# Moving the release points of streamed weights in the recurrent attention layer (layer A)

## The chip, the cores and the metric

The kernel runs on one core of a Trainium2 chip. The metric is the device time of one execution in microseconds (us). Three timed runs of the kernel before gave 3307.75, 3314.41 and 3315.86 us; the median is 3314.41 us. A further execution was taken with the hardware profiler; it is the one whose rows are shown.

## What is computed

Four layers run in the order A, B, A, B over 2048 rows of 640 numbers, each after a layer norm and with a residual sum. Layer A is the one that the change touches. It goes through the rows in segments of 32; each segment reads eight memory rows that the segment before it wrote, so the segments of a layer can only run one after the other:

```
for s in range(n_seg):                       # 64 segments of 32 rows
    h = concatenate([mem, xs])               # 8 memory rows + 32 rows of this segment
    q, k, v = h @ Wq, h @ Wk, h @ Wv         # 640 -> 32 heads of 192 each
    p = softmax(mask(q @ k.T * scale))
    o = (p @ v) @ Wo                         # 32 x 192 -> 640
    mem = o[:8]                              # read by the next segment
    outs.append(o[8:])
```

Wq, Wk, Wv and Wo have 640 x 6144 bf16 numbers each. Layer B is a linear attention over all rows with products of 640 columns; the change doesn't touch it.

## The kernel before

**Rounds.** The 32 heads are worked in four rounds of eight heads. `rounds(s)` runs through them forwards in even segments and backwards in odd ones, so the last round of one segment is the first of the next. In each round n TensorE projects queries, keys and values (`project`, three calls a round: Q0, K0, V0 up to V3 below), computes scores, attends, and multiplies by Wo (`wo_round`). A projection is five steps, one for each 128 of the 640 inputs, and each step is four matmuls on the four column groups of the array, twenty matmuls in all. Layer A's order is written out by hand (`manual_schedule`): every engine runs its instructions in the order of the code. On TensorE a segment runs Q0, K0, V0, then for n = 0, 1, 2: Q(n+1), scores, in n = 1 the first two thirds of an output round (`step` is its last matmul, L1281), K(n+1), attend, V(n+1); then output steps, scores of the last round, more output steps, attend, the other output steps, and at the end `wo_round` of the last round, whose sum gives the next segment's memory rows through VectorE (L1344, L1346).

**Weights.** Not all weights of layer A fit in SBUF beside the rest. Most pieces stay there (`res`). For the last and the first round of a segment, some pieces share a place: the slots, three for Q, two for K and two for V (`SLOTS`), hold the piece of one outer round at a time, and `wo_both` holds the larger part of Wo for either outer round. So in every segment eleven loads bring in the weights of its last round: Q2, Q3, Q4, K3, K4, V3, V4 (384 KB each, `load_slot`, L710; the number is the step of the projection that reads it) and four pieces of Wo (320 KB each, `load_piece`, L755). In the first round a projection takes its slot pieces first, and then they may be overwritten.

**Releases.** The loads are issued by SyncE (SP), whose queue is in order. To bound how many are under way, each load is held back in a list, `held`, and made to wait for a named matmul by a dependency that `release` adds (from L740):

```
def release(step, n=1):
    for load in held[:n]:
        tc.add_manual_dep(load().ins, step.ins.name, ...)
    del held[:n]
```

`project` appends the loads of its slots in round 0 and, at its end, releases one load behind its last matmul (L1077). `load_both` appends the four pieces of Wo after the output round of n = 1, and one more is released behind that round's last matmul (L1288). So the eleven loads wait in turn for the ends of Q0, K0, V0, Q1, K1, V1, Q2, of the output round, and of K2, V2 and Q3. In a layer's last segment (s = 63) eight pieces of Wo are held, since the next layer A wants another part kept; five of them are released at once behind the output round (L1284), ahead of two fetches of 1.5 MB (`fetch_tails`, L1357).

**Small transfers.** GpSimd issues the small loads of each round (extra keys and queries, L1043, and extra rows of V, L1054) and the stores. All transfers run on the same 16 DMA engines of the core.

Of the kernel before, what the change touches and what calls it, by code (L numbers as in the profile page):

```python
# [24 lines left out]
SEG_FILL = 1  # L25

VH = 194

STEPS = (2, 5)

# [4 lines left out]
def ap3(ap, dims):  # L35
    return bass.AP(tensor=ap.tensor, offset=ap.offset, ap=[list(d) for d in dims])
# [86 lines left out]
class Kernel:  # L123
# [540 lines left out]
    def layer_A(self, xn_dram, at_dram, li, x_raw=None):  # L664
# [5 lines left out]
        self.kqb_d = dram.tile([NR, P, NSEG, 192], BF16, name=f"kqb{li}")  # L670
        self.vb_d = dram.tile([NSEG, NR, 2, 8, 4 * VH], BF16, name=f"vb{li}")
        self.otb_d = dram.tile([P, NSEG, 384], BF16, name=f"otb{li}")
# [114 lines left out]
    def two_heads(self, ap):  # L787

        d = [list(x) for x in ap.ap]
        return ap3(ap, [d[0], [VH, 2], [1, 192]])  # L790

    def A_pre(self, xn_dram, li, load_matrix, piece, wo_mid, wo_end, lay_out_wo, early_wo, x_raw):
# [10 lines left out]
        sts = [wo_mid[:, 6144 * i:6144 * i + 192 * SH].rearrange("p (s f) -> p s f", f=192) for i in range(2)]  # L803
        vts = [wo_end[:, 8 * VH * i:8 * VH * i + 8 * VH].rearrange("p (g f) -> p g f", f=2 * VH) for i in range(2)]
        with ExitStack() as es:
# [176 lines left out]
    def A_chain(self, xn_dram, at_dram, li, load_slot, piece, late_wo, load_both, wo, low):  # L982
# [3 lines left out]
        with tc.tile_pool(name=f"A{li}_ch", reuse_waits="tile", bufs=1) as sp, \  # L986
# [5 lines left out]
            psq, psk = [pqp.tile([P, 512], F32, name=f"ps_qk_{m}") for m in "qk"]  # L992
            Vs = [sp.tile([P, 4 * VH], BF16, name=f"Vp{i}") for i in range(2)]
            xr = sp.tile([P, 160], BF16, name="xr")
# [16 lines left out]
            def rounds(s):  # L1011
                return range(NR) if s % 2 == 0 else range(NR - 1, -1, -1)
# [43 lines left out]
            def project(hT, ps, m, n, s, steps):  # L1056
                order = rounds(s)
                r = order[n]
                ns = SLOTS[m]
                for i in steps:  # L1060
                    b = (i + KC - ns) % KC if n == 0 else i
                    w = piece(m, r, b)
                    for g in range(4):
                        if m == "V":
                            hp = 2 * (g % 2) + g // 2
                            rhs = w[:, 384 * hp:384 * hp + 384]
                        else:
                            w3 = w[:, 32 * g:32 * g + 32]
                            rhs = ap3(w3, [list(w3.ap[0]), [P, 6], [768, 2], [1, 32]])
                        o = ps[32 * g:32 * g + 32, 0:384]  # L1070
                        if m != "V":
                            o = ps[32 * g:32 * g + 32, :].rearrange("p (x c) -> p x c", x=2)[:, :, 64 * (g // 2):64 * (g // 2) + 192]
                        last = nc.tensor.matmul(o, lhsT=hT[:, b, :], rhs=rhs, start=(i == 0),  # L1073
                                         stop=(i == KC - 1), tile_position=(0, 32 * g), skip_group_check=True)
                    if n == 0 and b >= KC - ns:
                        self.held.append(lambda b=b: load_slot(m, order[NR - 1], b))
                self.release(last)  # L1077

            def values(hT, n, s, pv, steps):
                project(hT, pv, "V", n, s, steps)  # L1080
# [9 lines left out]
            def turn_rows(pairs):  # L1090
                for o, i in pairs:
                    nc.vector.transpose(out=o, in_=i)  # L1092

            def v_rows(pv, n, engines):
                for x in range(2):
                    o = self.two_heads(Vs[n % 2][0:64, 2 * VH * x:2 * VH * x + 2 * VH])
                    i = pv[64 * x:64 * x + 64, 0:384].rearrange("p (e f) -> p e f", e=2)
# [17 lines left out]
            def attend(E, n):  # L1115
                O = [pop.tile([P, 512], F32, name="ps_o", tag="o0")] * 2
                if n == NR - 1:
                    O[1] = pop.tile([P, 512], F32, name="ps_o1", tag="v")
                V = Vs[n % 2]
                for G in range(2) if n < NR - 1 else (1, 0):  # L1120
                    for h in range(4):
                        nc.tensor.matmul(O[G][32 * h:32 * h + 32, VH * G:VH * G + 193], lhsT=E[0:80, 80 * h + 32 * G:80 * h + 32 * G + 32],  # L1122
                                         rhs=V[0:80, VH * h:VH * h + 193], start=True, stop=True, tile_position=(0, 32 * h),
                                         skip_group_check=True)
                if n % 2 == 0:
                    pair[0] = pop.tile([P, 512], F32, name="ps_t", tag="o1")
                q, m = (48, 32) if n % 2 == 0 else (64, 16)
                for h in range(4):
                    nc.tensor.matmul(pair[0][32 * h:32 * h + m, 0:193], lhsT=E[0:80, 80 * h + q:80 * h + q + m],  # L1129
                                     rhs=V[0:80, VH * h:VH * h + 193], start=True, stop=True, tile_position=(0, 32 * h),  # L1130
                                     skip_group_check=True)
                return O
# [28 lines left out]
            def turn_tail(rows, otb):  # L1161
                self.chain_end = [nc.vector.transpose(out=otb, in_=rows[:])]
                return otb
# [4 lines left out]
            def wo_round(W, r, OT, first, last, part=range(12)):  # L1168
                for i in part:
                    for g in range(2):  # L1170
                        q = 32 * (2 * (i % 2) + g)
                        rhs = wo[r, i].rearrange("p (a g f) -> p a g f", a=2, g=2)[:, :, g, :]
                        step = nc.tensor.matmul(W[q:q + 32, 0:320], lhsT=OT[i // 6][:, i % 6 // 2, 32 * (i % 2):32 * (i % 2) + 32],  # L1173
                                         rhs=rhs, start=(first and i < OWN + 2), stop=(last and i > 9), tile_position=(0, q),
                                         skip_group_check=True)
                return step
# [11 lines left out]
            def weigh():  # L1188
                S = scores()
                E = sp.tile([P, 320], BF16, name="E", tag="E")  # L1190
                nc.scalar.activation(out=E[0:80, 0:320], in_=S[0:80, 0:320], func=ACT.Exp, scale=scale)  # L1191
                return E
# [3 lines left out]
            def next_kq(s, n):  # L1196

                at = NR * s + n + 1
                if at < len(turns):
                    extra_kq(kqs.pop(0))  # L1200
# [19 lines left out]
            for s in range(NSEG):  # L1220
# [4 lines left out]
                def q_or_k(m, n, halves=False):  # L1225
                    ps = psk if m == "K" else psq
                    project(hT, ps, m, n, s, range(KC))
                    return to_rows(ps, m, halves)
# [44 lines left out]
                for n in range(L):  # L1273
                    raw = q_or_k("Q", n + 1)
                    if n == 2:
                        otb = turn_tail(otr, ots[0][:, 128:320])
                    E = weigh()
                    next_kq(s, n)
                    turn_rows(raw)
                    if n == 1:  # L1280
                        step = wo_round(W, order[0], OTs[0], True, False, range(OWN, 12))  # L1281
                        if s == NSEG - 1:
                            load_both(order[L], True)
                            self.release(step, 5)  # L1284
                            tails = [self.fetch_tails(tb, low) for tb in range(2)]
                        else:
                            load_both(order[L], False)
                            self.release(step)  # L1288
                    raw = q_or_k("K", n + 1, n + 1 == L)
                    O = attend(E, n)  # L1290
                    tails_after(n)
                    fetch_kq(s, n)
                    if n == 2:
                        store_tail(otb, s, order[1])
                    rc = weigh_rows(O)
                    if n == 1:
                        rct = weigh_tail()
                    turn_rows(raw)
                    pv = v_banks()
                    project(hT, pv, "V", n + 1, s, range(KC))  # L1300
                    osc = sp.tile([P, 384], BF16, name="osc", tag="raw")
                    for G in range(2):
                        scaled(osc[:, 192 * G:192 * G + 192], O, rc, G, "s")
                    turn(n, osc)
                    v_rows(pv, n + 1, "sv")
                    if n == 1:
                        otr = tail_rows(rct, "OTh")
# [22 lines left out]
                output_steps(len(outs))  # L1330
                if s == NSEG - 1:
                    self.first_tails = tails, [self.spread_tails(0, tails[0], low, "vvss")]
                if s + 1 < NSEG:
                    if s + 2 < NSEG:
                        load_rows(s + 2)
# [99 lines left out]
```

## Time and profile before

| what | value |
|---|---|
| median of three runs | 3314.41 us |
| profiled execution, its own time | 3309.64 us |
| its span, first to last instruction | 3307.9 us |
| granted TensorE clock, mean | 0.989 |
| busy: PE, PEld, DVE, ACT, POOL | 94%, 60%, 68%, 56%, 43% of the span |
| DMA traffic | 747.58 MB, mean 226 GB/s |
| loads of Wq, Wk, Wv and of laid-out Wo by SP | 427, 298, 290 and 560 |

How to read its rows: PE is TensorE's matmuls, PEld its weight loads, DVE VectorE, ACT ScalarE, POOL GpSimd, SP SyncE; L1073 is line 1073 of the kernel before. A row of the timeline gives the start and the duration in us, the engine, line and operation, the tile written and the tiles read, the shapes, the count of merged instructions, and in brackets the engine's idle time before it with what ended it. "issue" there means that the profile shows nothing that the engine waited for. A tile's name is that of the whole buffer: `arena` is the SBUF buffer that holds the weights.

### The profile page before, as it was taken

What the parts mean: (1) busy time and instruction counts of PE and PEld (TensorE: products, weight loads), DVE (VectorE), ACT (ScalarE), POOL (GpSimd) and SP (SyncE); (2) the same over time, 40 slices, a digit from 0 to 9 for tenths busy, and PEclk for the clock granted to TensorE, in tenths of its full rate; (3) what the DMA queues carried; (4) which work ended last, traced back from release to release, by engine and by line L of the source; (5) the groups of instructions that cost most, each with busy time, mean ns of one, the idle gap of its engine ahead of it and who ended that gap; (6) DMA issues with size and microseconds to landing.
All of it is one profiled execution on the core that took longest, in us unless ns stands there. A gap on an engine that the chain in (4) does not pass through costs nothing.

```text
span 3307.9 us, 141147 instructions
## 1 busy us (share of the span) xinstructions
PE 3097.4 (94%) x59424; PEld 1976.7 (60%) x59730; DVE 2265.7 (68%) x5711; ACT 1837.0 (56%) x4353; POOL 1423.4 (43%) x2926
## 2 busy tenths in 40 slices
PE   9889999999999999899999899999999999998999
PEld 7656666666666656555367566656666656665553
DVE  5457777777777777656643577777777777776565
ACT  3246666566565656536433466656665656665363
POOL 3344555555455555430122355545555554554300
PEclk9999999999999999999999999999999999999999
DMA  8987777777676777840385677777776777778300
GB/s 309 330 293 238 260 233 257 238 248 252 234 262 233 256 241 245 279 144 1 111 314 192 235 247 252 232 243 250 241 258 231 257 239 238 261 239 284 128 1 33
DMA packets 325236, 747.58 MB, mean 226 GB/s; under 512 B 66066, under 2 KB 100490, under 8 KB 321530
## 3 DMA queue, kind: packets, MB, share of 16 engines
q1 hardware_dynamic: 254586, 638.46, 54.9%
q0 software_dynamic: 67808, 86.77, 9.1%
q10 hardware_dynamic: 2208, 13.30, 1.0%
q8 instruction: 469, 7.68, 1.0%
q14 instruction: 165, 1.35, 0.1%
HBM read 668.78 MB, written 77.00 MB: 225 GB/s over the span
## 4 chain that ended last, share of the span: by engine, by line
PE 70%; DMA 13%; DVE 10%; issue 4%; ACT 2%; POOL 1%; SPq 0%; PEld 0%; ACTq 0%; DVEq 0%; POOLq 0%
PE ps_qk_q L1073 12%; PE ps_qk_k L1073 11%; PE ps_v L1073 10%; PE ps_w L1173 10%; DMA arena<-in_A_Wv_dram 6%; PE ps_s L1109 5%; PE ps_pre L941 4%; DMA Vp<-vb 4%; PE ps_o L1122 2%; DVE wt L1344 2%; PE kv L1390 2%; PE ps_pre L968 2%; PE ps_wo L429 2%; DVE hT L1346 2%; PE ps_pq L480 1%
## 5 line engine op out<-in xcount | busy, mean ns | idle before, releaser
L1073 PEld LDWEIGHTS <-hT 128*32 128x32 bf16 x30720 | 787.8, 97 | 440.4 <-issue 56.2
L1092 DVE STREAM_TRANSPOSE QK<-raw 128x512 bf16<-128x512 bf16 (+1 forms) x1152 | 730.4, 643 | 214.8 <-ACT raw L1087 159.1
L1073 PE MATMUL ps_qk_q<-arena,hT 128*32 128x384 bf16 x10240 | 509.6, 327 | 57.0 <-DVE hT L1346 38.6
L1050 POOL COPY QK<-kqb 64x192 bf16<-64x192 bf16 x1024 | 349.9, 342 | 395.3 <-PE ps_s L1109 357.5
L1073 PE MATMUL ps_qk_k<-arena,hT 128*32 128x384 bf16 x10240 | 511.9, 329 | 3.2 <-ACT raw L1087 1.0
L1087 ACT ACTIVATE raw<-ps_qk_k 128x512 bf16<-128x512 f32 (+1 forms) x640 | 313.6, 511 | 257.6 <-PE ps_qk_k L1073 257.5
L1073 PE MATMUL ps_v<-arena,hT 128*32 128x384 bf16 x8192 | 438.0, 327 | 16.7 <-DMA arena<-in_A_Wv_dram 14.2
L1054 POOL DMA_DIRECT2D Vp<-vb x512 | 258.7, 505 | 439.3 <-PE ps_t L1129 431.3
L1147 ACT ACTIVATE osc<-ps_o,rc 128x192 bf16<-128x192 f32 x896 | 334.4, 422 | 116.8 <-DVE rc L1141 112.2
L1087 ACT ACTIVATE raw<-ps_qk_q 128x512 bf16<-128x512 f32 x512 | 305.7, 597 | 165.4 <-PE ps_qk_q L1073 150.7
L1173 PE MATMUL ps_w<-arena,under 128*32 128x320 bf16 x6144 | 307.8, 301 | 12.9 <-issue 12.7
L1101 DVE CAST Vp<-ps_v 64x384 bf16<-64x384 f32 x512 | 286.2, 559 | 35.3 <-ACT Vp L1099 20.4
L1043 POOL DMA_DIRECT2D kqb<-kqb x512 | 293.1, 572 | 36.0 <-issue 25.8
L1109 PEld LDWEIGHTS <-QK 128*80 128x80 bf16 x4096 | 195.8, 121 | 159.4 <-issue 157.9
L1099 ACT ACTIVATE Vp<-ps_v 64x384 bf16<-64x384 f32 x512 | 246.4, 481 | 52.4 <-PE ps_v L1073 52.1
L1109 PE MATMUL ps_s<-QK 128*80 128x80 bf16 x4096 | 256.4, 210 | 3.4 <-issue 3.1
L1032 ACT ACTIVATE wh<-ps_w 64x160 f32<-64x160 f32 x256 | 76.9, 300 | 328.3 <-DVE wt L1344 269.1
L1191 ACT ACTIVATE E<-ps_s 80x320 bf16<-80x320 f32 x512 | 218.0, 426 | 34.5 <-PE ps_s L1109 34.3
L1039 POOL DMA_DIRECT2D attn<-under x128 | 91.9, 718 | 324.3 <-DVE under L1035 321.1
L941 PEld LDWEIGHTS <-arena 128*128 128x128 bf16 x1920 | 189.0, 99 | 40.5 <-DMA arena<-in_A_Wk_dram 10.0
L94 DVE CAST arena<-ps_pre 128x512 bf16<-128x512 f32 (+1 forms) x160 | 102.3, 647 | 154.2 <-PE ps_pre L941 107.1
L1122 PE MATMUL ps_o<-Vp,E 80*32 80x193 bf16 x4096 | 179.9, 248 | 19.4 <-DMA Vp<-vb 9.6
(159 smaller groups left out, 4643.8 us busy)
## 6 DMA issues: line engine op xcount, KB each, us to landing
arena<-wo_rows SPq DMA_DIRECT2D x560, 320.0 KB, 6.0
arena<-in_A_Wq_dram SPq DMA_DIRECT2D x427, 384.0 KB, 4.2
arena<-in_A_Wk_dram SPq DMA_DIRECT2D x298, 384.0 KB, 5.3
arena<-in_A_Wv_dram SPq DMA_DIRECT2D x290, 384.0 KB, 5.5
kqb<-kqb POOLq DMA_DIRECT2D x512, 48.0 KB, 4.6
vb<-arena POOLq DMA_DIRECT2D x128, 97.0 KB, 6.0
Vp<-vb POOLq DMA_DIRECT2D x512, 24.2 KB, 4.5
kqb<-arena SPq DMA_DIRECT2D x8, 1536.0 KB
```

Of the source, the lines that this page charges most:

```text
L941: nc.tensor.matmul(ps[:, T * i:T * i + T], lhsT=w[b][:, P * c:P * c + P], rhs=xBT[:, b, :], start=(b == 0), stop=(b == KC - 1))
L1043: nc.gpsimd.dma_start(out=kqb[:], in_=self.kqb_d[r, :, s, :])
L1050: nc.gpsimd.tensor_copy(out=o, in_=kqb[h, :].rearrange("p (x c q) -> p x c q", c=3, q=16))
L1054: nc.gpsimd.dma_start(out=Vs[n % 2][64:80, :], in_=self.vb_d[s, r].rearrange("g t f -> (g t) f"))
L1073: last = nc.tensor.matmul(o, lhsT=hT[:, b, :], rhs=rhs, start=(i == 0), stop=(i == KC - 1), tile_position=(0, 32 * g), skip_group_check=True)
L1087: nc.scalar.activation(out=raw[:, c], in_=ps[:, c], func=ACT.Copy)
L1092: nc.vector.transpose(out=o, in_=i)
L1099: nc.scalar.activation(out=o, in_=i, func=ACT.Copy)
L1101: nc.vector.tensor_copy(out=o, in_=i)
L1109: nc.tensor.matmul(S[0:80, c0:c0 + 80], lhsT=KT[:, 4 * x + c, :], rhs=QT[:, 4 * x + c, :], start=(c % 2 == 0), stop=(c % 2 == 1), skip_gro ...
L1147: nc.scalar.activation(out=out, in_=i, func=ACT.Copy, scale=rc[G])
L1173: step = nc.tensor.matmul(W[q:q + 32, 0:320], lhsT=OT[i // 6][:, i % 6 // 2, 32 * (i % 2):32 * (i % 2) + 32], rhs=rhs, start=(first and i ...
```

## The change

A table, `PACE`, names for each projection the step behind which one load is released; a projection that is not in the table releases none. The release after the output round of n = 1 is dropped, and in the last segment eight loads are released there instead of five. Only the steps that the loads wait for change: the loads, their order on SP and all matmuls stay.

```diff
+PACE = {("Q", 0): 0, ("K", 0): 3, ("Q", 1): 1, ("K", 1): 1, ("V", 1): 3, ("Q", 2): 4, ("K", 2): 0, ("V", 2): 3, ("Q", 3): 4,
+        ("K", 3): 3, ("V", 3): 4}
...
                     if n == 0 and b >= KC - ns:
                         self.held.append(lambda b=b: load_slot(m, order[NR - 1], b))
-                self.release(last)
+                    if PACE.get((m, n)) == i:
+                        self.release(last)
...
                         if s == NSEG - 1:
                             load_both(order[L], True)
-                            self.release(step, 5)
+                            self.release(step, 8)
                             tails = [self.fetch_tails(tb, low) for tb in range(2)]
                         else:
                             load_both(order[L], False)
-                            self.release(step)
...
+                assert not self.held
```

In the order of the loads the eleven steps before are the ends of Q0, K0, V0, Q1, K1, V1, Q2, the output round, K2, V2 and Q3. After the change they are step 0 of Q0, step 3 of K0, step 1 of Q1, step 1 of K1, step 3 of V1, step 4 of Q2, step 0 of K2, step 3 of V2, step 4 of Q3, step 3 of K3 and step 4 of V3. Step 4 is the end of a projection. In the built program eight more matmuls in each segment signal a semaphore in the middle of a projection, and the one at the end of the output round no longer does.

## Prediction

> **What bounds the kernel now.** The first part of the page has TensorE busy for 94% of the span, and the shares of the chain that ended last give PE 70% and DMA 13%. The two chains of layer A (64 segments each) are most of the span, so I cut the trace at the first query matmul of each segment and read one segment in the timeline of TensorE (start, us, engine, line, tiles, count, idle before and what ended it). This segment starts at 1335.06.
>
> ```profile
> 1335.06 1.00 PE L1073 MATMUL ps_qk_q<-arena,hT 128*32 128x384 bf16 x20 [0.29 <-DVE hT L1346]
> ...
> 1346.94 1.05 PE L1073 MATMUL ps_v<-arena,hT 128*32 128x384 bf16 x16
> 1348.46 0.35 PE L1073 MATMUL ps_v<-arena,hT 128*32 128x384 bf16 x4 [0.47 <-DMA arena<-in_A_Wv_dram]
> ...
> 1351.61 0.44 PE L1173 MATMUL ps_w<-arena,QK 128*32 128x320 bf16 x5
> 1353.25 0.86 PE L1173 MATMUL ps_w<-arena,QK 128*32 128x320 bf16 x19 [1.19 <-issue]
> ...
> 1355.25 1.00 PE L1073 MATMUL ps_qk_q<-arena,hT 128*32 128x384 bf16 x20 [0.41 <-DVE hT L1346]
> ```
>
> It took 20.19 us and shows the two losses: the last four V matmuls wait for a streamed V piece, and five matmuls into the last output round TensorE stops for 1.19 us for nothing that the profile names. By the starts of all segments (124 inside the two chains), the shortest is 18.01 us, the median 18.69, the mean 18.77. In the median segment nothing moves before the third round: V3 (values of round 3) starts at 11.88 us in at least three quarters of them. So 0.75 us per segment, some 92 us in all, is lost behind that point, and only that can be won.
>
> Why there? The table of windows cuts one segment (306.84 to 325.15) into stretches; the last two columns are the DMA share and GB/s.
>
> ```profile
> 306.80:308.80 2.00, 1.96 (x48) 1.30 (x52) 1.46 (x5) 1.37 (x4) 0.78 (x2) 1.00 0.06 20
> ...
> 317.80:320.80 3.00, 3.00 (x76) 2.14 (x72) 2.69 (x8) 2.37 (x8) 1.84 (x5) 1.00 1.04 384
> 320.80:323.80 3.00, 2.77 (x84) 1.87 (x73) 1.95 (x7) 0.75 (x2) 2.51 (x6) 1.00 0.29 91
> ```
>
> The rings stand empty for the first 2 us, are full to about 14 us, and are nearly empty again. The stream is late by its late start. The queues and issues of the page tell the rest (KB each, median us from issue to landing):
>
> ```profile
> q8 instruction: 469, 7.68, 1.0%
> ...
> arena<-wo_rows SPq DMA_DIRECT2D x560, 320.0 KB, 6.0
> ...
> arena<-in_A_Wv_dram SPq DMA_DIRECT2D x290, 384.0 KB, 5.5
> ```
>
> The 469 instruction packets of 16 KB are TensorE's code: its 119,154 matmuls and weight loads by 469 are 254 each, so a packet is a block of 256. Of the 49 waits of TensorE over 0.45 us within the chains that no other engine ended, 46 stand at one and the same place of the 256: they are waits for code. The waits by releaser (us in total, times, longest) give the sizes:
>
> ```profile
> PE ps_w L1173 <- issue: 36.8, 48, 1.7
> ...
> PE ps_v L1073 <- DMA arena<-in_A_Wv_dram: 14.2, 33, 0.9
> ...
> PE ps_o L1122 <- DMA Vp<-vb: 9.6, 23, 1.2
> ```
>
> From starts of matmuls, I count 41 us in code waits over 0.3 us, 23 us for V pieces (54 segments), some 8 us for Vp rows.
>
> Code comes late when weights are queued. For each block I took the time from its boundary to the end of the next block's packet, by the number of weight loads issued and not landed: with 0 or 1 it is 1.7 to 2.0 us (median), with 3 or 4 it is 3.1 to 3.2 (95% below 3.9), with 5 it is 3.9, with 6 4.2, with 7 5.4. TensorE crosses a boundary no earlier than 1.2 us after the packet's end, and a block lasts 5.1 to 6.3 us. So waits need over 3.9 us: 48 of 49 happened with 5 or more under way, one in 261 blocks with fewer.
>
> **The change part by part.** No matmul, byte or SP order of a steady segment changes; eleven releases move. An issue follows its releasing step by 0.2 us (1.04 us for one whose last matmul ends near 0.85), and a step of a projection is 153 ns. So, in us from the segment's start:
>
> | load | issued | landed, median | issued after (worked out) | needed by TensorE |
> |---|---|---|---|---|
> | Q2 | 1.04 | 4.40 | 0.42 | 9.78 |
> | Q3, Q4 | 1.85, 2.67 | 5.90, 7.70 | 1.70, 3.02 | 9.95, 10.11 |
> | K3, K4 | 3.48, 4.83 | 8.86, 10.01 | 4.37, 5.75 | 11.30, 11.46 |
> | V3, V4 | 5.90, 6.71 | 11.19, 12.47 | 6.71, 8.00 | 12.37, 12.53 |
> | Wo pieces 0 to 3 | 7.80, 8.61, 9.68, 10.49 | 13.48, 14.66, 15.71, 16.54 | 9.53, 10.49, 11.70, 12.91 | 16.16, 16.29, 16.43, 16.56 |
>
> Service: landings of Q2 to the last piece are (16.54 - 4.40) / 10 = 1.21 us apart; new issues are (12.91 - 0.42) / 10 = 1.25 apart. A load that finds the rings empty (Q2) lands 3.35 us after issue, 4.45 at the 95th percentile. So the new stream just keeps up, with about 3 under way instead of 5 to 6. Then:
>
> 1. **V4** lands at 8.00 + 3.35 to 4.45 = 11.35 to 12.45, before its need at 12.53. Its waits go: 23 us. What is late next: a segment without a V wait has a fixed 0.2 us between scores and the next output steps that a V wait swallows; 54 times 0.2 = 11. Net -12.
> 2. **Code**: with 3 to 4 under way 3.1 us, so nearly all of the 41 us go; I keep 4. Net -37.
> 3. **Vp rows**: these come by GpSimd's queue on the same engines; bounds 0 and -8, I take half, -4.
> 4. **Smaller waits** of the same stretch (several of 0.1 to 0.3 us behind a late block of code) are the rest of the 92, 20 us. Segments with none of the counted waits (28) have median 18.23, mean 18.31, so the rest does not all go: bounds 0 and -20, I take -11.
> 5. **Last Wo piece**: new issue 12.91, landing 3.2 to 4.45 later (as Q2, a little less for its 320 KB), 16.1 to 17.4, need 16.56. About 0.13 us per segment on the mean, times 126 = +16. Nothing hides it: behind it stand the last matmuls and the hand-over to the next segment.
> 6. **Signals**: eight more matmuls per segment signal SP in mid projection. The first matmul behind a signalling one starts 153 ns after the step before, like steps without one (151 to 163): 0, at most 8 x 128 x 10 ns = 10.
> 7. **SP**: each of its waits still ends in the order of TensorE's own program; SP has nothing else queued in a chain but the two 1.5 MB fetches of each last segment. There eight pieces are released instead of five; the bytes ahead of the last piece stay, so the 8.4 us that TensorE waits for it stay. 0, between -2 and +2 per layer.
>
> Sum: -12 - 37 - 4 - 11 + 16 = -48 against the profiled execution's 3309.6 us (span 3307.9): 3262. The runs' median is 3314.4, 5 above; I take 3263.
>
> [...]
>
> **Rivals.**
> - *All of it goes.* Every segment near the fastest (18.05): -0.72 x 126 = -91, 3219 to 3225. For: the last piece waits in only 5 of 117 segments now. Against: its issue moves 2.4 us later.
> - *Code waits stay*, since it matters that some load is under way and not how many. Then V gives -12, the last piece, with TensorE late anyway, takes back 8: 3306. For: at 3 or 4 it is still 1.2 us more than at 0. Against: 1 wait in 261 blocks.
> - *The last piece becomes the bound* and it is slower. The gross gain is 64 us, 0.51 per segment; the piece breaks even when it lands 12.91 + x = 16.56 + 0.51, that is x = 4.2 us after its issue. If the 5.0 us that Q4 took holds for it, it stalls 1.35 x 126 = 170: 3309.6 - 64 + 170 = 3416. For: 1.25 against 1.21 leaves 3% of room, and GpSimd's small transfers come at 14 to 16 us. Against: 6.0 us today is queueing behind five others; with two it should be near 3.4.
>
> **How the numbers follow.** Forecast 62% (own range 3235 to 3290); all goes 14%; code waits stay 14%; last piece 10%. Measurement tells 0.3%, 10 us. Faster: 62 + 14 + 4 of the third = 80%; within 0.3%: 10 of the third, 1 of the fourth, 11%; slower 9%. The range 3222 to 3312 takes in the third case and most of the second and leaves out the last.
>
> **What would show it.** Right: segment median near 18.3; V waits gone from the waits by releaser; issue waits of ps_w under 8 us; landing medians of V and Wo loads from 5.5 and 6.0 to under 4.5; a new wait of ps_w on wo_rows of some 10 to 20 us beside the two long ones. Wrong: code waits as many at fewer loads under way, or that new wait above 60 us.

## The result and the profile after

The changed kernel took 3358.54 us (median of four runs, 3354.99 to 3362.50), the kernel before in the same comparison 3311.08 us (four runs, 3304.76 to 3315.86). The ratio is 1.015, with a 95% interval of 1.013 to 1.017: it is slower by 1.5%. I had forecast 3263 us, faster. The profiled execution of after took 3362.50 us, span 3360.8 us; against the profiled execution of before, 3309.64 us, it is 52.9 us longer at a clock of 0.987 (before 0.989), a difference of 0.2% that could account for some 7 us at most. One profiled execution of those below, that of experiment 13, took 9811.5 us where its other runs took about 3260, and none of its rows are used.

First the queues and the issues of the page (KB each, median us from issue to landing):

```profile
q8 instruction: 469, 7.68, 0.9%
...
arena<-wo_rows SPq DMA_DIRECT2D x560, 320.0 KB, 4.7
arena<-in_A_Wq_dram SPq DMA_DIRECT2D x427, 384.0 KB, 4.0
arena<-in_A_Wk_dram SPq DMA_DIRECT2D x298, 384.0 KB, 4.5
arena<-in_A_Wv_dram SPq DMA_DIRECT2D x290, 384.0 KB, 5.0
```

The same code and the same loads; each load is under way for less time (V 5.0 us after, 5.5 before; Wo 4.7 after, 6.0 before). Fewer loads are queued at once, as meant: when V4 is issued, 2.9 others are under way on the mean, where it was 4.2. But 5.0 and 4.7 are not the 3.35 to 4.45 us with which I had reckoned. The waits of TensorE by releaser (us in total, times, longest) show what that does:

```profile
PE ps_w L1177 <- DMA arena<-wo_rows: 77.6, 106, 8.1
PE ps_v L1076 <- DMA arena<-in_A_Wv_dram: 46.9, 76, 1.5
...
PE ps_w L1177 <- issue: 2.4, 5, 1.2
```

The wait of ps_w for code ("issue") has fallen from 36.8 us in 48 waits to 2.4 in 5. In its place TensorE waits for the last Wo pieces 106 times, and the wait for V pieces, which was to go, has grown from 14.2 us to 46.9. By starts of matmuls, as I counted before: code 3.3 us in 6 waits (40.8 in 49 before), V pieces 62.7 us in 100 segments (23.6 in 54), Wo pieces 79.3 us in 115 segments (0.3 in 5), Vp rows none (8). The sum is +39 + 79 - 37.5 - 8 = +72; the 52.9 that were measured leave some -20 to small waits that I don't count one by one.

The profile's own idle times give a second count of the code waits: idle time of over 0.3 us before a matmul of the two chains, put down to "issue". It has 45.4 us in 55 waits before and 4.9 us in 8 after. The code waits of the experiments are counted in this second way.

One segment in the timeline of TensorE, from 307.18 to 326.58 (19.40 us long):

```profile
319.06 0.82 PE L1076 MATMUL ps_v<-arena,hT 128*32 128x384 bf16 x16
320.38 0.35 PE L1076 MATMUL ps_v<-arena,hT 128*32 128x384 bf16 x4 [0.50 <-DMA arena<-in_A_Wv_dram]
...
323.53 0.92 PE L1177 MATMUL ps_w<-arena,QK 128*32 128x320 bf16 x20
325.12 0.32 PE L1177 MATMUL ps_w<-arena,QK 128*32 128x320 bf16 x4 [0.67 <-DMA arena<-wo_rows]
325.25 1.02 PE L1184 MATMUL ps_idle<-arena,ident 128*32 128x512 bf16 x4
326.58 1.00 PE L1076 MATMUL ps_qk_q<-arena,hT 128*32 128x384 bf16 x20 [0.30 <-DVE hT L1350]
```

The last four V matmuls wait 0.50 us, the last four output matmuls 0.67 us, and 1.46 us after these start the next segment begins. The chain of waits of the same stretch (start, us, what) shows the two as one chain:

```profile
315.12 0.02 issue
315.14 5.20 DMA arena<-in_A_Wv_dram
320.34 0.04 issue
320.38 0.37 PE ps_v L1076 x4
320.75 0.02 issue
320.77 4.30 DMA arena<-wo_rows
325.07 0.04 issue
325.12 0.34 PE ps_w L1177 x4
```

The V piece takes 5.20 us; the end of V3, which waited for it, releases the last Wo piece, which takes 4.30 us; then TensorE goes on. From 315.12 to 325.12, half the segment, no engine's work is on the chain but 0.37 us. In the shares by engine of the page the DMA has 27%, where it had 13%:

```profile
PE 62%; DMA 27%; DVE 6%; issue 2%; ACT 1%; POOL 0%; SPq 0%; PEld 0%; DVEq 0%; ACTq 0%; POOLq 0%
```

A plain rule comes out of the landings of all 124 segments: in after, a segment ends 1.50 us behind the landing of its last Wo piece (5th percentile 1.50, 95th 1.58). That landing is at 17.66 us on the mean, 17.66 + 1.50 = 19.16, and the mean segment takes 19.18. So the question is why the eleventh load lands at 17.54 us (median) when the first one is issued 0.65 us earlier than before, and the last one landed at 16.54 before.

### The profile page after: what moved, and what is told of

Its sections match the earlier page's. It is cut to its first block, busy times and chain, and to the rows that moved or that the text cites. A ratio compares the mean times of both kernels' runs of the same rounds, so it can differ in the third digit from the quotient of the medians.

```text
span 3360.8 us, 141173 instructions
## 1 busy us (share of the span) xinstructions
PE 3118.5 (93%) x59458; PEld 1974.4 (59%) x59730; DVE 2264.6 (67%) x5711; ACT 1839.1 (55%) x4353; POOL 1422.7 (42%) x2926
## 3 DMA queue, kind: packets, MB, share of 16 engines
q1 hardware_dynamic: 254586, 638.46, 55.9%
q0 software_dynamic: 67808, 86.77, 10.2%
## 4 chain that ended last, share of the span: by engine, by line
PE 62%; DMA 27%; DVE 6%; issue 2%; ACT 1%; POOL 0%; SPq 0%; PEld 0%; DVEq 0%; ACTq 0%; POOLq 0%
DMA arena<-wo_rows 13%; DMA arena<-in_A_Wv_dram 13%; PE ps_qk_q L1076 11%; PE ps_qk_k L1076 10%; PE ps_v L1076 10%; PE ps_w L1177 5%; PE ps_pre L944 5%; PE ps_s L1113 4%; PE ps_pre L971 2%; PE kv L1394 2%; DVE wt L1348 2%; PE ps_wo L432 2%; DVE hT L1350 2%; PE ps_pq L483 1%; PE ps_o L1126 1%
## 5 line engine op out<-in xcount | busy, mean ns | idle before, releaser
L1076 PE MATMUL ps_v<-arena,hT 128*32 128x384 bf16 x8192 | 445.2, 328 | 48.8 <-DMA arena<-in_A_Wv_dram 46.9
L1177 PE MATMUL ps_w<-arena,QK 128*32 128x320 bf16 x3072 | 154.1, 303 | 91.5 <-DMA arena<-wo_rows 77.6
```

## Theories

The trace has 16 arrivals for each of these loads; a ring, in this document, is what brings one of the 16.

**Theory of the rings run dry** (G in the expectations, F where it says that V4 is late by what is ahead of it). A spacing that is even on the average (1.25 us between issues, as worked out) is not enough. Where a release comes a little late, the rings move less (after 0.15 MB between 7 and 8 us of a segment, before 0.33), and that is not made up afterwards: after is 0.2 MB behind at 8 us and 0.3 MB behind at 12. This theory was formed last, and only experiments 7 and 10 were run to try it. **Rivals:** the late release of the last pieces alone does it (theory A below); the rings deliver the same bytes at the same rate whenever they are asked (B); loads behind V4 delay V4 (E); or the small transfers of GpSimd take the rings (C, against D). Each is tried.

In the experiments the table holds a tuple of steps for each projection and one load is released for each entry; the label that the expectations use stands in brackets, and each diff shows the entries that differ from after. The loads always come in the order Q2, Q3, Q4, K3, K4, V3, V4, Wo 0 to 3. Lag means the time from issue to landing, and landing that of the last of the 16 rings; times without another word are medians over the 124 segments, from the segment's start. "By releaser" means the rows of waits; other waits are counted from starts of matmuls. Experiments 4, 5 and 6 leave out loads or halve them, so their results are not those of the layer.

## Experiments: which half of the change is at fault

**1 (e1). The first seven releases as in after, Wo nearly as in before.**

```diff
-("K", 2): (0,), ("V", 2): (3,), ("Q", 3): (4,), ("K", 3): (3,), ("V", 3): (4,)
+("K", 2): (0, 0, 4), ("V", 2): (4,), ("Q", 3): (4,)
```

> The changed kernel, with the first seven loads (Q2 to V4) paced as changed, and the four Wo pieces released nearly as before: two loads behind step 0 of K2 (V4 and Wo piece 0), then the ends of K2, V2 and Q3. Theory A (a load lands 4.2 to 5.0 us after its issue with three to four under way, so the late issues are what TensorE waits for): the 79 us of waits for Wo pieces go, the 63 us of V waits stay, code waits come back by 5 to 15 us; 3285 to 3300 us. Theory B (the rings deliver the same bytes at the same rate whenever they are asked, and the last piece is late for that): within 10 us of the changed kernel's 3358.

Measured: 3402.82 us, ratio 1.028 (1.024 to 1.032), the slowest of all. The waits of TensorE:

```profile
PE ps_v L1075 <- DMA arena<-in_A_Wv_dram: 109.8, 120, 3.4
...
PE ps_w L1176 <- DMA arena<-wo_rows: 31.3, 28, 7.9
PE ps_w L1176 <- issue: 18.8, 24, 2.2
```

By releaser the wait for Wo pieces falls from 77.6 to 31.3 us, as theory A has it, and the wait for V pieces doubles, from 46.9 to 109.8. The time lies in neither theory's range. V4 is issued at 7.96 us as in after, but now two Wo pieces are issued right behind it, and it lands at 13.49 instead of 12.92. The last piece lands at 17.54, the same as in after, though it is issued 2.9 us earlier (10.49). Theory A falls as the whole account: here the release time of the last piece didn't set its landing.

**2 (e2). The reverse: the first seven as in before, Wo as in after.**

```diff
-("Q", 0): (0,), ("K", 0): (3,), ("Q", 1): (1,), ("K", 1): (1,), ("V", 1): (3,), ("Q", 2): (4,), ("K", 2): (0,)
+("Q", 0): (4,), ("K", 0): (4,), ("V", 0): (4,), ("Q", 1): (4,), ("K", 1): (4,), ("V", 1): (4,), ("Q", 2): (4,)
```

> The other half: the first seven loads released as in the kernel before, the four Wo pieces as in the changed one (the last behind the end of V3). Theory A: the last piece lands after 12.9 + 4.2 = 17.1 us or later, 0.5 us after its need, so 60 to 80 us of Wo waits appear; V waits stay near 23 us and code waits fall from 41 to about 25; 3335 to 3370 us. Theory B: 3311 within 10.

Measured: 3340.39 us, ratio 1.012 (1.009 to 1.016). This is theory A's range. V waits 18.7 us, Wo waits 78.3, code 7.5. Here the last piece is released at 13.00 and lands at 17.32: so late, the lag of 4.0 us is enough for the loss even where V waits no more than before (23.6). By the ratios each half of the change loses by itself, 93 us (experiment 1) and 41 us, and both together 50: they do not add up, so they are not two separate losses.

**3 (e3). The early start alone.**

```diff
+PACE = {("Q", 0): (0,), ("K", 0): (4,), ("V", 0): (4,), ("Q", 1): (4,), ...}
```

This diff is against before; all releases but the first stay at the ends of their steps.

> The kernel before with one release moved: the first load behind step 0 of Q0 in place of its end, 0.65 us earlier. Theory A: with the rings full from then on, all later loads land up to 0.6 us earlier; V waits fall from 23 to under 10 us, code waits stay at 35 to 45 us; 3290 to 3305 us. Theory B' (the start has no worth, since the second to the eleventh load are issued as before): 3311 within 5.

Measured: 3302.49 us, ratio 0.999 (0.997 to 1.000): nothing that can be told. Q2 lands earlier and V4 at 12.48 us, as before (12.47). One load put 0.65 us ahead, with the next one where it was, opens a hole behind itself: between 3 and 4 us the rings move 0.10 MB, where before they moved 0.32 (means over the segments).

## Experiments: whose bytes and whose time

**4 (e6). Half the bytes.** All eleven loads fetch half their columns; the releases are those of after.

```diff
-                self.last_load = nc.sync.dma_start(out=slot[m, b], in_=wview[m][:, b, PW * r:PW * r + PW])
+                self.last_load = nc.sync.dma_start(out=slot[m, b][:, 0:n], in_=wview[m][:, b, PW * r:PW * r + n])
...
+            n = 1280 if into is wo_kept else 640
+            self.last_load = nc.sync.dma_start(out=into[:, c:c + n], in_=self.wo_rows[r, :, own + c:own + c + n])
...
-                        self.held.append(lambda b=b: load_slot(m, order[NR - 1], b))
+                        self.held.append(lambda b=b: load_slot(m, order[NR - 1], b, 768))
```

> The changed kernel with the streamed loads cut to half their columns (the other half keeps older weights, so the result is another). The same signals, releases and counts. If the waits are bytes (theories A and D): V and Wo waits go, and what is left is a segment near 18.05 us; 3215 to 3235 us. If a fixed time per load from issue to landing made them (4 us and more whatever its size): the last piece still lands after 16.6 and over 30 us of Wo waits stay; 3260 us or more. If the signals in mid projection cost something: the shortest segment is above 18.01 us by eight times that cost.

Measured: 3221.70 us, ratio 0.976 (0.973 to 0.978). The shares of the chain by engine, then the issues of V loads:

```profile
PE 83%; DVE 9%; DMA 4%; issue 2%; ACT 1%; POOL 0%; SPq 0%; DVEq 0%; ACTq 0%; PEld 0%; POOLq 0%
```
```profile
arena<-in_A_Wv_dram SPq DMA_DIRECT2D x256, 192.0 KB, 2.9
```

The DMA falls from 27% of the chain to 4%, and a halved V load lands 2.9 us after its issue instead of 5.0. The V waits are 0.5 us, code waits none, and the segments take 18.02 us in the median, 18.016 in the shortest (before: 18.014). So it is bytes that were late; and eight more matmuls that signal in each segment, with all the new release points in place, cost nothing.

**5 (e5). No small loads.** From the second segment on GpSimd's extra keys and queries are set to zero and the extra V rows aren't loaded; the releases are those of after.

```diff
+                if s > 0:
+                    nc.gpsimd.memset(kqb[:], 0.0)
...
+                if s > 0:
+                    return
```

> The changed kernel without GpSimd's small loads of each round: from the second segment on the extra keys and queries are set to zero in place and the extra rows of V are left as they are, so these parts of the result are not computed. Theory C (the small transfers hold up one ring of the sixteen, whose last share then lands 1.0 to 1.4 us behind the median): the lag of the last ring falls under 0.6 us, V4 lands near 12.2 in place of 12.9, the last Wo piece near 16.6 in place of 17.5; 3280 us or less. Theory D (the loads slow themselves; the small ones are 10% of the rings): lags within 0.3 us of now, 3335 to 3360 us.

Measured: 3311.26 us, ratio 1.002 (1.000 to 1.004), between the two theories. The V waits fall from 62.7 to 36.6 us and the Wo waits from 79.3 to 54.7: the small loads cost some 47 us in after (3358.54 less 3311.26), and the page counts GpSimd's queue (q0, 10.2% in after) and SP's (q1, 55.9%) as shares of the same 16 engines. But most of the waits stay, and the last ring still lands about 1 us behind the median one.

**6 (e10). No Wo pieces at all.** In all segments but a layer's last the four pieces aren't loaded, so nothing is queued behind V4.

```diff
-                            load_both(order[L], False)
+                            pass
```

> The changed kernel without the four Wo pieces in all but each layer's last segment (the last round multiplies by older Wo numbers, so the result is another); seven loads are left, released as in the changed kernel. Theory E (the rings serve all loads under way at once, so loads issued behind V4 delay it): V4 lands near 12.4 to 12.6 in place of 12.92 and its waits fall from 63 to under 35 us. Theory F (V4's landing is set by what was issued ahead of it): V4 lands within 0.15 us of 12.92 and its waits stay at 55 us or more. No Wo waits in either; E 3240 to 3265 us, F 3275 to 3295.

Measured: 3270.82 us, ratio 0.989 (0.987 to 0.991). The waits of TensorE:

```profile
PE ps_v L1075 <- DMA arena<-in_A_Wv_dram: 43.7, 71, 2.0
```

V4 lands at 12.90 us, as in after (12.92), and its waits stay (43.7 and 46.9 us by releaser). The time lies between the two ranges, but the landing and the waits are those of theory F. Theory E falls at this spacing: V4 is late by what happens ahead of it. With two pieces issued right behind V4 (experiment 1) it was later by 0.57 us, so loads behind it can count.

## Experiments: where the rings run dry

The windows answer where. Columns: stretch, its length, busy time of PE, PEld, DVE, ACT and POOL with counts, PE clock, DMA share, GB/s. First before, in a segment that begins at 306.84, from 4 to 10 us of it:

```profile
310.84:313.84 3.00, 3.00 (x80) 1.99 (x72) 2.38 (x5) 2.21 (x7) 1.67 (x4) 1.00 1.05 385
313.84:314.84 1.00, 1.00 (x31) 0.76 (x32) 0.87 (x2) 0.69 (x2) 0.68 (x2) 1.00 0.94 347
314.84:316.84 2.00, 2.00 (x64) 1.39 (x60) 1.12 (x5) 1.38 (x4) 0.87 (x2) 1.00 1.04 345
```

Then after, in a segment that begins at 403.70, the same stretches, and 14 to 16.5 us:

```profile
407.70:410.70 3.00, 3.00 (x80) 2.00 (x72) 2.38 (x5) 2.21 (x7) 1.67 (x4) 1.00 0.98 366
410.70:411.70 1.00, 1.00 (x31) 0.75 (x32) 0.87 (x2) 0.69 (x2) 0.68 (x2) 1.00 0.78 154
411.70:413.70 2.00, 2.00 (x64) 1.40 (x60) 1.11 (x5) 1.38 (x4) 0.87 (x2) 1.00 0.94 344
...
417.70:420.20 2.50, 2.39 (x74) 1.64 (x75) 2.14 (x7) 0.89 (x3) 1.70 (x5) 1.00 0.80 252
```

Between 7 and 8 us of the segment the rings move 154 GB/s where before they moved 347. By the packets of SP's queue over all segments (medians), both kernels have moved the same by 6 us (after 1.17 and before 1.18 MB of 4.06), after 0.15 MB and before 0.33 MB between 7 and 8, and 1.26 and 1.36 MB from 8 to 12. The hole is that of K4: it is released at 5.74 us, 1.39 behind K3, where before it came at 4.83. What is missing at 8 us (0.2 MB) and at 12 (0.3 MB) is not made up, and so the rings still move 252 GB/s at the end of the segment, when before they had nearly nothing left. It is not the only gap: between 12 and 13 us after moves 0.26 MB and before 0.33.

**7 (e13). K4 alone released earlier,** at the end of K1 instead of step 3 of V1. V4 is released as late as in after.

```diff
-("K", 1): (1,), ("V", 1): (3,)
+("K", 1): (1, 4)
```

> The changed kernel with one release moved: K4 behind step 4 of K1 (issue 4.83) in place of step 3 of V1 (5.74). V4 and the last Wo piece keep their steps. Theory G (the rings run empty at 7 to 8 us because K4 comes late, and are behind from there to the end): K4 lands near 9.7 in place of 10.2, V4 near 12.5 in place of 12.9 though it is released as late as before, V waits fall from 63 to 20 to 30 us, Wo waits from 79 to 60 to 70; 3305 to 3325 us. If the release of V4 and of the last piece themselves set it: V4 within 0.15 us of 12.92, 3345 to 3360 us.

Measured: 3327.99 us, ratio 1.006 (1.004 to 1.008). The window of 7 to 8 us (this segment begins at 402.15) and of 14 to 16.5:

```profile
409.15:410.15 1.00, 1.00 (x31) 0.75 (x32) 0.87 (x2) 0.69 (x2) 0.69 (x2) 1.00 1.05 393
...
416.15:418.65 2.50, 2.38 (x72) 1.61 (x65) 1.91 (x7) 0.52 (x2) 2.13 (x6) 1.00 0.77 248
```

The hole is closed (393 GB/s), and V4, issued at 7.96 us as in after, lands at 12.54 instead of 12.92; the V waits halve, from 62.7 to 29.5 us. One release of another load 0.9 us earlier, and 31 us gone: for V4 this is the experiment that shows the mechanism. For the last piece it does not: the Wo waits stay (80.8 us, where theory G had 60 to 70), the piece is released at 12.98 and lands at 17.28, and the time is 3 us above the theory's range.

**8 (e12). Only the last pieces earlier** (Wo 2 and 3 at steps 0 and 3 of K3).

```diff
-("K", 3): (3,), ("V", 3): (4,)
+("K", 3): (0, 3)
```

> The changed kernel with its last two Wo pieces released earlier, behind steps 0 and 3 of K3 (issue near 11.1 and 11.7 us) in place of step 3 of K3 and the end of V3; V4 and all before as changed. They come behind most of V4's bytes. If the late issue of the last piece makes its wait: it lands near 16.4, Wo waits fall from 79 to 15 to 30 us, V waits stay at 60 to 70; 3295 to 3315 us. If the waits only change places as in the kernel with all four pieces early: V waits rise by 30 us or more and the total stays above 3335.

Measured: 3338.75 us, ratio 1.011 (1.009 to 1.012). The last piece is issued 1.7 us earlier than in after (11.68) and lands 0.18 earlier (17.36). The waits:

```profile
PE ps_w L1176 <- DMA arena<-wo_rows: 57.7, 82, 7.9
PE ps_v L1075 <- DMA arena<-in_A_Wv_dram: 51.7, 79, 1.7
```

Neither branch came as expected. By releaser the Wo waits fall by 20 us, to 57.7 and not to 15 to 30, so the late issue is a small part of them; the V waits rise by 5 us and not by 30, so the waits don't just change places. The bytes moved by 8 us (1.66 MB) and by 12 us (2.93 MB) are the same as in after.

**9 (e11). The last release freed from V4's wait** (step 2 of V3, ahead of the matmuls that wait for V4).

```diff
-("V", 3): (4,)
+("V", 3): (2,)
```

> The changed kernel with the last Wo piece released behind step 2 of V3 in place of step 4, so that the wait for V4, which stands at step 4, no longer holds its release back. If that coupling matters: its issue comes at 12.6 to 12.7 in place of 13.4, it lands 0.6 us earlier, and Wo waits fall from 79 to 35 to 50 us; 3315 to 3335 us. If the rings decide when it lands: landing within 0.2 us of 17.54, 3345 to 3360 us.

Measured: 3344.57 us, ratio 1.013 (1.010 to 1.015). Issued at 12.59 instead of 13.37 and landed at 17.48 instead of 17.54. So the chain that the profile draws (V wait, release, Wo piece) is true but explains little: without its link the rings deliver the piece 0.06 us earlier in the median and 0.13 in the mean, and the kernel is 14 us faster, less than a third of what the change lost.

**10 (e14). Both: K4 and the last pieces earlier.**

```diff
-("K", 1): (1,), ("V", 1): (3,), ... ("K", 3): (3,), ("V", 3): (4,)
+("K", 1): (1, 4), ... ("K", 3): (0, 3)
```

> The same with the last two Wo pieces behind steps 0 and 3 of K3, as in the run that moved only these and saved 20 us against the changed kernel. Theory G: now that the rings are not behind, the earlier issue counts: the last piece lands near 16.7, Wo waits fall to 15 to 30 us; 3265 to 3290 us. If the two act apart from each other: e13 less 20 us.

Measured: 3315.29 us, ratio 1.002 (1.000 to 1.004): theory G's 3265 to 3290 was missed, and the other branch (the two act apart, 20 us below experiment 7) is nearer, with 13. The last piece lands at 17.21 us; V4 and Wo 0, still issued at 7.96 and 9.52, reach the median ring at 11.50 and 12.56 us, against 10.56 and 11.40 in experiment 14 below. One hole is closed and another follows: between 8 and 11 us the rings move 0.81 MB in experiments 7 and 10, where they move 0.96 in after and 0.97 in experiment 14. Of the 0.21 MB that the earlier K4 had gained by 8 us, 0.07 are left at 12. One late release less is not enough; V4 and Wo 0 were still released late.

## Experiments: other paces, and a better one

**11 (e4). A middle pace:** early start, Q4 to V4 within 0.2 us of their issues before, Wo spread out.

```diff
+("Q", 0): (0,), ("K", 0): (2,), ("V", 0): (4,), ("Q", 1): (4,), ("K", 1): (4,), ("V", 1): (3,), ("Q", 2): (4,),
+("K", 2): (0,), ("V", 2): (2,), ("Q", 3): (4,), ("K", 3): (2,)
```

> A pace between the two, spaced 1.1 us: Q2 behind step 0 of Q0, Q3 step 2 of K0, Q4, K3, K4 the ends of V0, Q1, K1, V3 step 3 of V1, V4 the end of Q2, Wo pieces step 0 of K2, step 2 of V2, the end of Q3, step 2 of K3 (issue near 11.5 us). Theory A: V4 lands near 11.8 and the last piece near 16.1, so both waits are under 15 us each, with code waits of 10 to 20 us: 3255 to 3285 us. Theory B: 3300 or above.

Measured: 3250.39 us, ratio 0.983 (0.981 to 0.985). The time lies just below theory A's range. V waits 12.1 us, Wo 4.2, code 11.4. V4 is issued at 6.71 us, the last piece at 11.52, landing at 16.42.

**12 (e7). V4 earlier still.**

```diff
+("Q", 0): (0,), ("K", 0): (1,), ("V", 0): (2,), ("Q", 1): (2,), ("K", 1): (2,), ("V", 1): (1,), ("Q", 2): (2,),
+("V", 2): (0, 4), ("Q", 3): (4,), ("K", 3): (2,)
```

> The middle pace with the first seven loads one to two steps earlier and the first two Wo pieces about one us later: Q2 step 0 of Q0, Q3 step 1 of K0, Q4 step 2 of V0, K3 step 2 of Q1, K4 step 2 of K1, V3 step 1 of V1, V4 step 2 of Q2, Wo pieces steps 0 and 4 of V2, the end of Q3, step 2 of K3. If loads issued behind V4 take bandwidth from it (as the half with two releases at once suggests: V4 landed 0.6 us later there), V4 lands near 12.0 in place of 12.4 and its waits fall under 8 us: 3235 to 3248 us. If V4's landing is set by the bytes ahead of it alone: 12.3, 3250 within 6.

Measured: 3260.07 us, ratio 0.987 (0.984 to 0.990). V4 lands at 11.93 us and the V waits fall to 2.1, as the first branch has it, but code takes 14.8 and Wo 8.6: what V gave, the others took, and the time lies above both ranges.

**13 (e9). An even pace with an earlier end.**

```diff
+("Q", 0): (0,), ("K", 0): (2,), ("V", 0): (3,), ("Q", 1): (3,), ("K", 1): (3,), ("V", 1): (2,), ("Q", 2): (3,),
+("K", 2): (4,), ("V", 2): (2,), ("Q", 3): (3,), ("K", 3): (1,)
```

> A pace between the two best so far, to see how much of the waits is left to win: Q2 step 0 of Q0, Q3 step 2 of K0, Q4 step 3 of V0, K3 step 3 of Q1, K4 step 3 of K1, V3 step 2 of V1, V4 step 3 of Q2, Wo pieces the end of K2, step 2 of V2, step 3 of Q3, step 1 of K3. V4 near 12.2, the last piece near 16.3; V and Wo waits under 20 us together, code waits 8 to 12 us: 3240 to 3252 us. If these waits trade against each other in any pace, 3250 to 3262.

Measured: ratio 0.986 (0.984 to 0.988), 3255.59 to 3264.47 us in four runs: the range of the second branch, that the waits trade against each other in any pace, and a little above.

**14 (e15). Dense first, then wide:** the first seven about 1 us apart, Wo as in experiment 11.

```diff
+("Q", 0): (0,), ("K", 0): (1,), ("V", 0): (2,), ("Q", 1): (2,), ("K", 1): (2,), ("V", 1): (1,), ("Q", 2): (2,),
+("K", 2): (0,), ("V", 2): (2,), ("Q", 3): (4,), ("K", 3): (2,)
```

> The first seven loads as in e7 (V4 behind step 2 of Q2), the Wo pieces as in e4 (step 0 of K2, step 2 of V2, the end of Q3, step 2 of K3). V waits under 6 us as in e7, Wo waits under 8 as in e4, code waits 10 to 15 as the price of the denser first half: 3240 to 3252 us. If the three trade against each other: 3250 to 3262.

Measured: 3239.02 us (3234.59 to 3240.65), ratio 0.979 (0.977 to 0.981): faster than both kernels. Windows of 7 to 8 us and 14 to 16.5 us (the segment begins at 302.46):

```profile
309.46:310.46 1.00, 1.00 (x31) 0.74 (x32) 0.87 (x2) 0.68 (x2) 0.68 (x2) 1.00 1.01 387
316.46:318.96 2.50, 2.38 (x72) 1.60 (x68) 1.91 (x7) 0.52 (x2) 2.12 (x6) 1.00 0.34 107
```

The rings are full at 7 us and done by 16. The waits of TensorE for weights and code in the last round:

```profile
PE ps_w L1176 <- DMA arena<-wo_rows: 5.5, 9, 1.2
...
PE ps_w L1176 <- issue: 4.1, 10, 0.8
```

The median segment takes 18.02 us, the mean 18.17; V4 is issued at 6.39 and lands at 12.10, the last piece at 11.52 and 16.12. The three waits didn't trade against each other here: code takes 6.0 us, where 10 to 15 were expected.

**15 (e8). No pacing,** for the other end: seven loads within the first 3.4 us, all four Wo pieces behind the output round.

```diff
+("Q", 0): (0, 1, 2), ("K", 0): (0, 1), ("V", 0): (0, 1)
...
+                            self.release(step, 4)
```

> The opposite pole: every load released as soon as its place is free (Q2 to Q4 behind steps 0, 1, 2 of Q0, K3 and K4 behind steps 0, 1 of K0, V3 and V4 behind steps 0, 1 of V0, all four Wo pieces behind the output round), so up to seven are under way from 2 us on. If code waits grow with the loads under way: 60 us or more of them, at earlier places of the segment; V waits under 10 us, Wo waits none; 3290 to 3340 us. If they do not depend on the number: 41 us or fewer of code waits and 3270 to 3285 us.

Measured: 3358.16 us, ratio 1.018 (1.014 to 1.022). The issue of V loads, then the waits of TensorE:

```profile
arena<-in_A_Wv_dram SPq DMA_DIRECT2D x290, 384.0 KB, 8.1
```
```profile
PE ps_w L1176 <- issue: 40.9, 42, 1.9
...
PE ps_o L1125 <- DMA Vp<-vb: 15.6, 25, 1.9
PE ps_o L1125 <- issue: 11.1, 15, 1.5
PE ps_s L1112 <- issue: 9.6, 10, 1.9
```

Hardly a wait for V (1.8 us by starts of matmuls) and none for Wo in the chains, but 85.1 us in 95 waits for code, and 15.6 us for Vp rows. That is the branch by which code waits grow with the loads under way: 60 us or more, and earlier, with 37 of the 95 ahead of 12 us in the segment, where before had none. All 81 that are over 0.45 us stand at one and the same place of the 256, and all 95 end 1.2 to 1.6 us behind the end of a code packet, as before. The time lies above the range. It is as slow as after, for the opposite reason: the rings move at least 0.28 MB in every microsecond from 2 to 13 us (mean), and code and Vp rows come late beside that (85.1 and 15.6 us of waits).

**All paces side by side.** The bytes moved by 14 us go with the landing of the last piece. In before and experiments 3, 11, 12 and 14 they are 3.80 to 3.91 MB, and it lands at 16.1 to 16.5 us; in after and experiments 1, 2, 5 and 7 to 10 they are 3.50 to 3.58 MB, and it lands at 17.1 to 17.5; in experiment 15 it is 4.02 MB and 15.56 us. The release time of that piece goes from 10.49 to 13.37 us within the late group. This is a count that fits theory G, not one more experiment.

## Why the prediction was wrong, point by point

- **Where the time can be won** (behind V3): right. Experiments 4 and 14 bring the median segment to 18.02 us.
- **Step 2, code** (-37): right, 40.8 to 3.3 us, -37.5 (by the second count 45.4 to 4.9, -40.5). The time of a code packet goes with the number of loads under way. In after, the packet ends 1.0 us behind the boundary with no load under way, 2.3 with two, 3.1 with five (medians); in experiment 15, 3.9 with five and 4.6 with seven. By the second count there are 8 code waits in after, 55 before and 95 in experiment 15. So the rival "code waits stay" falls.
- **Step 3, Vp rows** (-4): the whole 8 us went.
- **Step 4, smaller waits** (-11): by the remainder some -20, my far bound; not measured singly.
- **Step 1, V4** (-23 of waits, -12 net): wrong, +39. This is the step that failed first. It took the lag from Q2, a load that finds the rings empty: 3.35 to 4.45 us. V4's lag was 4.96 us, with three loads still under way ahead of it, so it landed at 12.92 where the need was at 12.53. The prediction's own table had the nearer rows: before the change Q3, with one load ahead, took 4.05 us and Q4, with two, 5.03. The sentence behind it, "the new stream just keeps up", set the mean spacing of 1.25 us beside the mean service of 1.21. The means are right and the conclusion is not: the issues up to K4 came 1.30, 1.30, 1.36 and 1.39 us apart, each more than 1.21, so the rings ran short between 7 and 8 us (0.15 MB for 0.33), and a later spacing of 0.97 (K4 to V3) did not give back what was not moved. Experiment 7 shows it: K4 0.9 us earlier, V4 0.38 earlier.
- **Step 5, last Wo piece** (+16): right in kind, five times too small, +79. Issue 13.37 instead of 12.91, because V4's wait delays V3; the lag from there was 4.15, inside the 3.2 to 4.45 that I gave. Experiment 9 shows that undoing the later issue brings the landing forward by 0.06 us only, since the lag grows to 4.87: a lag that is added to an issue time is the wrong sum for a piece that finds the rings behind. That the deficit of bytes is the rest is argued from the counts; no experiment closed all of the gaps and left this release late.
- **Step 6, signals** (0): right, by the shortest segment of experiment 4.
- **Step 7, last segments** (0): right as far as the profile shows: the longest Wo wait is 8.1 us where I said 8.4.

The rival that came true is the third, the last piece becomes the bound, to which I gave 10%. I had its break-even at 4.2 us behind 12.91; it came 4.63 behind (17.54). Put into that rival's own sum: 3309.6 - 64 + (17.54 - 16.56) x 126 = 3369, against 3362.5 measured. That closeness is partly luck: the 64 holds 12 us for V waits, which grew by 39 instead. My argument against the rival was that "with two" ahead the lag should be near 3.4; the piece had three ahead of it, small loads beside them, and a last ring 1.0 to 1.4 us behind the median one. Of the signs that I named, one came as said (issue waits of ps_w 2.4 us, under 8); the segment median is 19.06 and not 18.3, the V loads' 5.0 and the Wo loads' 4.7 us are above 4.5, and "that new wait above 60 us" stands in the waits with 77.6.

## What to carry to other kernels

Here a stream that had to be done by a given time was late by its idle moments (0.15 MB for 0.33 between 7 and 8 us) though its mean spacing, as worked out, sufficed (issues 1.25 us apart, landings before the change 1.21). So count the bytes that the rings have moved by each time, and compare curves, before comparing issue spacing with service time. Two limits stand against each other here, rings that run dry (79.3 us of Wo waits in after) and many loads under way, beside which code comes late (85.1 us of code waits in experiment 15); the best pace put the first seven loads about 1 us apart and the last four wider (0.979), while too wide (1.015) and none at all (1.018) cost the same. And the lag of a load has to be read at the number of loads that will be under way (V4 in after 4.96 us with three), not from one that found the rings empty (Q2 before 3.35).

## What the runs showed of the hardware

- The last of the 16 rings lands V4 1.0 to 1.6 us behind the median ring (after 12.92 against 11.69, experiment 14 12.10 against 10.56), Q2 in empty rings only 0.35 (after), and TensorE waits for the last one: in after, the matmuls that waited over 0.3 us for a V piece (57) or a Wo piece (75) start 0.04 us behind the 16th arrival. A code packet between issue and landing goes with about half a microsecond of it: in after, 1.13 us for loads with one (993 loads), 0.54 for those without (371). The small loads explain little (V4 in after 1.21 us, in experiment 5 1.02). What holds that ring back is open.
- Lag against depth, for 384 KB: 3.2 to 3.4 us into empty rings; 3.9 to 5.0 with two or three loads ahead still under way (after, Q4 to V4); 5.7 with four ahead (before, V4); 8.2 with six ahead (experiment 15, V4). The 320 KB pieces took 6.0 us with five ahead (before), and 192 KB takes 2.4 to 3.05. While loads are queued, the stream runs at some 0.33 MB a microsecond (from 8 to 12 us 1.36 MB in before, 1.26 in after).
- A wait that the chain of the profile draws between two late loads need not be their cause: cutting it (experiment 9) moved the landing by 0.06 us (median).
